# Gating the later loads and interleaving halves of the first V sums with the transposes, in a fused attention and gated-MLP kernel

## The chip, the cores and the metric

One core of a Trainium2 chip runs the whole kernel. The metric is the device time in microseconds of one execution. TensorE (PE in the profile) does matrix products and transposes, VectorE (DVE), ScalarE (ACT) and GpSimd (POOL) do the elementwise work, and SyncE (SP) issues nearly all loads and stores.

## The reference

With x of 2048 tokens by 512 features, all in bfloat16:

```python
xn  = layernorm(x)                                # no scale, no bias, eps 1e-5
q, k, v = split(xn @ wqkv)                        # 32 heads of 16
s   = q @ k.T * 16 ** -0.5, kept where 0 <= i - j < 256
att = softmax(s) @ v @ wo
mlp = ((xn @ w_gate) * (xn @ w_up)) @ w_down      # inner width 1792
out = x + att + mlp
```

## The kernel before

The tokens are worked off in blocks of 128 and in chunks of four blocks. Everything stays on the chip between the loads at the start and the stores of the result. `run` writes the order of all engines out by hand: it calls `setup` and `first_chunk`, then goes through steps of scores (L317), exponentials (L323), masks and values (L370), and between them fills TensorE with projections, gate and up products (L399, L410), down products (L432) and the output product (L438) from a list.

`setup` issues all loads on SyncE's one queue in this order (L74 to L89): x of block 0, of block 1, of blocks 2 and 3; the V, K and Q columns of wqkv (L77, 512 KB each); the first halves of w_gate and w_up; x of blocks 4 to 7; the second halves; w_down; wo; the rest of x. It also calls `keep_busy(40)`, forty products of zeros into a PSUM tile `wps` (L131) that nothing reads, so that TensorE has something to do while the first x lands.

`first_chunk` does chunk 0 by itself. Per block b:

- `norm_stats` (L173, L174) and `norm_scale` (L183, L186) make mean and inverse deviation on VectorE and GpSimd; `norm_apply` (L194) writes the scaled block `xn` on VectorE, one instruction of 512 columns.
- `norm_transpose` (L213) transposes the four 128x128 parts of `xn` on TensorE into a PSUM tile `xTp`, and ScalarE copies them to `xnT` (L214). For block 0 the parts go two by two into two tiles with a copy each; for the others four into one tile with one copy.
- `proj_v` (L243) sums the four products of `xnT` with the V columns of wqkv into a PSUM tile `vp`, and VectorE or ScalarE copies it out to V (L236, L234).

Between the transposes of block 0 and those of block 1 stands `keep_busy(8)`. Then, for b from 0 to 3, the transposes of block b+1 are issued before the V sum of block b:

```python
for b in range(4):
    if b < 3:
        self.norm_transpose(b + 1, False)
    self.proj_v(b, engine="act" if b == 2 else "dve")
    if b == 0:
        self.norm_apply(3)
```

After V come the key and query sums (`proj_qk`, L255), the copy of V with its halves swapped (`swap_halves`, L153) and the list. PSUM tiles of `ps_m` (tag M, four buffers, `wps` among them) are taken in turn; the scores' tile S has four banks of its own.

Of the kernel before, what the change touches and what calls it, by code (L numbers as in the profile page):

```python
# [8 lines left out]
F32 = mybir.dt.float32  # L9
I32 = mybir.dt.int32  # L10
ACT = mybir.ActivationFunctionType
ALU = mybir.AluOpType
# [22 lines left out]
class Kernel:  # L35
# [26 lines left out]
    def setup(self):  # L62
        nc, const, NT, NF = self.nc, self.const, self.NT, self.NF
        self.x = const.tile([128, NT, 512], BF16, name="x")
        self.Wqkv = const.tile([128, 4, 1536], BF16, name="Wqkv")
        self.Wo = const.tile([128, 4, 512], BF16, name="Wo")
        self.Wg = const.tile([128, 4, self.F], BF16, name="Wg")
        self.Wu = const.tile([128, 4, self.F], BF16, name="Wu")
        self.Wd = const.tile([128, NF, 512], BF16, name="Wd")
        xv = self.x_d.rearrange("(t p) d -> p t d", p=128)  # L70
        wq = self.w_d["qkv"].rearrange("(k p) n -> p k n", p=128)
        wg = self.w_d["g"].rearrange("(k p) n -> p k n", p=128)
        wu = self.w_d["u"].rearrange("(k p) n -> p k n", p=128)
        for lo, hi in ((0, 1), (1, 2), (2, 4)):  # L74
            nc.sync.dma_start(out=self.x[:, lo:hi, :], in_=xv[:, lo:hi, :])
        for lo in (1024, 512, 0):
            nc.sync.dma_start(out=self.Wqkv[:, :, lo:lo + 512], in_=wq[:, :, lo:lo + 512])  # L77
        h = self.F // 2
        for lo in (0, h):
            nc.sync.dma_start(out=self.Wg[:, :, lo:lo + h], in_=wg[:, :, lo:lo + h])  # L80
            nc.sync.dma_start(out=self.Wu[:, :, lo:lo + h], in_=wu[:, :, lo:lo + h])
            if lo == 0:
                nc.sync.dma_start(out=self.x[:, 4:8, :], in_=xv[:, 4:8, :])
        nc.sync.dma_start(out=self.Wd[:], in_=self.w_d["d"].rearrange("(f p) n -> p f n", p=128))
        wo = self.w_d["o"].rearrange("(c p) n -> p c n", p=128)
        for c in range(4):
            nc.sync.dma_start(out=self.Wo[:, c, :], in_=wo[:, c, :])
        for lo, hi in ((8, 10), (10, 12), (12, NT)):
            nc.sync.dma_start(out=self.x[:, lo:hi, :], in_=xv[:, lo:hi, :])  # L89

        self.idle = const.tile([128, 128], BF16, name="idle")
        nc.vector.memset(self.idle[:], 0.0)  # L92
        self.keep_busy(40)
        warm = const.tile([128, 1], F32, name="warm")
        nc.vector.memset(warm[:], 0.0)
        nc.scalar.activation(out=warm[:], in_=warm[:], func=ACT.Exp)
        ident = const.tile([128, 128], BF16, name="ident")
        nc.gpsimd.memset(ident[:], 0.0)
        nc.gpsimd.affine_select(out=ident[:], in_=ident[:], compare_op=ALU.not_equal, fill=1.0,
                                base=0, pattern=[[-1, 128]], channel_multiplier=1)  # L100
        self.ident = ident
        pi = const.tile([128, 1], I32, name="pi")
        nc.gpsimd.iota(pi[:], pattern=[[0, 1]], base=0, channel_multiplier=1)
        podd = const.tile([128, 1], I32, name="podd")
        nc.vector.tensor_scalar(out=podd[:], in0=pi[:], scalar1=4, scalar2=1,
                                op0=ALU.arith_shift_right, op1=ALU.bitwise_and)
        self.odd = const.tile([128, 1], F32, name="odd")
        nc.vector.tensor_copy(out=self.odd[:], in_=podd[:])
        self.even = const.tile([128, 1], F32, name="even")
        nc.vector.tensor_scalar(out=self.even[:], in0=self.odd[:], scalar1=-1.0, scalar2=1.0,  # L110
                                op0=ALU.mult, op1=ALU.add)
        self.mhalf = const.tile([128, 4], F32, name="mhalf")
        nc.gpsimd.memset(self.mhalf[:], -0.5)
        self.diag = const.tile([128, 64], BF16, name="diag")
        self.far = const.tile([128, 64], BF16, name="far")
        nc.gpsimd.memset(self.diag[:], BIG)
        nc.gpsimd.memset(self.far[:], BIG)
        for half in (slice(0, 64), slice(64, 128)):
            self.triangle(self.diag[half], True)
            self.triangle(self.far[half], False)  # L120
        self.xnT, self.Q, self.hT, self.OT = {}, {}, {}, {}
        self.K, self.V, self.VS = {}, {}, {}
        self.strips, self.parts, self.at = {}, {}, {}
        self.stock = []
        self.new_values()

    def keep_busy(self, n):

        ps = self.ps_m.tile([128, 128], F32, tag="M", name="wps")
        for _ in range(n):  # L130
            self.nc.tensor.matmul(ps[:], lhsT=self.idle[:], rhs=self.idle[:], start=True, stop=True)  # L131

    def new_chunk(self, T):

# [55 lines left out]
    def norm_apply(self, t):  # L190
        nc = self.nc
        mv, j, rs = self.stats.pop(t)
        xn = self.work.tile([128, 512], BF16, tag="xn", name="xn")
        nc.vector.tensor_scalar(out=xn[:], in0=self.x[:, t, :], scalar1=mv[:, j, 0:1],  # L194
                                scalar2=rs[:, j:j + 1], op0=ALU.subtract, op1=ALU.mult)
        self.book("dve", MASK)
        self.xns[t] = xn

    def norm_transpose(self, t, by_dma):

        nc = self.nc
        xn = self.xns.pop(t)
        T, b = divmod(t, 4)
        if b == 0:
            self.xnT[T] = self.chunk2.tile([128, 4, 4, 128], BF16, tag="xnT", name=f"xnT{T}")
        if by_dma:
            nc.sync.dma_start_transpose(out=self.xnT[T][:, b, :, :], in_=xn[:])
            return
        n = 2 if b == 0 else 4
        for lo in range(0, 4, n):  # L210
            ps = self.ps_m.tile([128, n, 128], BF16, tag="M", name="xTp")
            for k in range(n):
                nc.tensor.transpose(ps[:, k, :], xn[:, 128 * (lo + k):128 * (lo + k) + 128], self.ident[:])  # L213
            nc.scalar.activation(out=self.xnT[T][:, b, lo:lo + n, :], in_=ps[:], func=ACT.Copy)  # L214

    def bank(self, ks, name):

# [54 lines left out]
    def first_chunk(self):  # L272

        self.new_chunk(0)
        for b in range(2):
            self.norm_stats(b, 1)
            self.norm_scale(b, 1)
        for b in (0, 1, 2):
            self.norm_apply(b)
            if b < 2:  # L280
                self.norm_stats(b + 2, 1)
                self.norm_scale(b + 2, 1)
        self.norm_transpose(0, False)
        self.keep_busy(8)
        for b in range(4):
            if b < 3:
                self.norm_transpose(b + 1, False)
            self.proj_v(b, engine="act" if b == 2 else "dve")
            if b == 0:
                self.norm_apply(3)  # L290
        self.proj_qk(0, 0, 1, engine="dve")
        self.proj_qk(0, 0, 0, engine="act")
        self.swap_halves(0, self.nc.scalar)
        self.proj_qk(0, 1, 1, engine="dve")
# [234 lines left out]

    def run(self):  # L530
        self.xns, self.stats, self.sums = {}, {}, {}
        self.pads = 0
        self.now, self.free = 0, dict(act=0, dve=0)
        self.setup()
        NCH = self.NCH
# [17 lines left out]
        spent, n = 0, 0  # L553
# [62 lines left out]
        T = NCH - 1  # L616
# [58 lines left out]
```

The softmax here doesn't subtract the row's maximum and nothing guards it: scores larger than these inputs give would overflow.

## Time and profile before

| | |
|---|---|
| median of 4 runs | 263.44 us (263.27 to 264.25) |
| profiled execution | 263.52 us |
| its span, first to last instruction | 261.5 us |
| TensorE busy | 257.8 us (99%) |
| VectorE, ScalarE, GpSimd busy | 179.5, 176.4, 115.7 us |
| bytes read from HBM | 9.70 MB |
| first V sum, first key sum on TensorE | 6.96, 11.05 us |

Times inside an execution count from its first instruction. A line of the timeline gives start, duration, engine, source line, operation, tile written and tile read, shapes, how many were merged, and in brackets the idle time before and what ended it. "L213" is line 213 of the listing. PE durations include a modelled end, so the distance of two starts, not the duration, is what a product costs in a dense row.

### The profile page before, as it was taken

How to read it: one execution, taken by the hardware profiler on the slowest of the kernel's cores; microseconds unless marked ns; L12 is line 12 of the kernel's file. 1: busy time of each engine (PE TensorE's matmuls, PEld its weight loads, DVE VectorE, ACT ScalarE, POOL GpSimd, SP SyncE). 2: the span in 40 equal slices, each digit the busy share in tenths (PEclk: the TensorE clock that was granted, in tenths of full speed). 3: DMA queues.
4: the chain of work that ended last, by engine and by line, in shares of the span. 5: the costliest groups of instructions: out<-in, count | busy, mean ns of one | idle time of the engine just before them, and what ended most of it. 6: DMA issues, size and time to landing. Idle time of an engine off the chain costs nothing.

```text
span 261.5 us, 7740 instructions
## 1 busy us (share of the span) xinstructions
PE 257.8 (99%) x3170; PEld 118.5 (45%) x3170; DVE 179.5 (69%) x357; ACT 176.4 (67%) x143; POOL 115.7 (44%) x278
## 2 busy tenths in 40 slices
PE   8999999999999999999999999999999999999995
PEld 8444444444444544444544454444544445444453
DVE  6687888879845597557973769767795235977344
ACT  3377788888756866678775567767787546787600
POOL 6215342425457645334456644544443451464600
PEclk9999999999999999999999999999999999999999
DMA  6999920120002300002001310001100100000002
GB/s 194 377 354 338 278 36 20 24 48 1 3 28 34 103 3 1 3 0 48 3 3 40 84 43 3 0 1 25 27 3 0 43 24 20 5 0 3 1 3 83
DMA packets 19427, 15.05 MB, mean 58 GB/s; under 512 B 7360, under 2 KB 19392, under 8 KB 19392
## 3 DMA queue, kind: packets, MB, share of 16 engines
q1 hardware_dynamic: 18848, 14.26, 18.4%
q8 instruction: 26, 0.43, 0.7%
q10 hardware_dynamic: 544, 0.30, 0.4%
q14 instruction: 9, 0.07, 0.1%
HBM read 9.70 MB, written 2.10 MB: 45 GB/s over the span
## 4 chain that ended last, share of the span: by engine, by line
PE 99%; DVE 0%; issue 0%
PE gp L399 19%; PE up L410 19%; PE psd L432 17%; PE qkp L255 11%; PE S L317 9%; PE acc L370 7%; PE vp L243 5%; PE psd L438 5%; PE L L432 2%; PE wps L131 2%; PE L L438 1%; PE xTp L213 1%; PE L L370 0%; DVE x L448 0%; DVE idle L92 0%
## 5 line engine op out<-in xcount | busy, mean ns | idle before, releaser
L323 ACT ACTIVATE P<-S 128x2048 bf16<-128x2048 f32 x75 | 140.7, 1876 | 49.6 <-PE S L317 41.0
L162 POOL TENSOR_SCALAR_AFFINE_SELECT P<-P 64x256 bf16<-64x256 bf16 x224 | 99.4, 444 | 124.4 <-ACT P L323 107.9
L399 PE MATMUL gp<-xnT,Wg 128*128 128x512 bf16 x224 | 60.1, 380 | 0.0
L410 PE MATMUL up<-xnT,Wu 128*128 128x512 bf16 x224 | 59.1, 380 | 0.0
L415 DVE TENSOR_TENSOR hT<-up,gsb 128x512 bf16<-128x512 f32 x56 | 38.3, 685 | 18.3 <-PE up L410 13.1
L432 PE MATMUL psd<-Wd,hT 128*128 128x512 bf16 (+1 forms) x210 | 48.0, 369 | 0.0
L347 DVE TENSOR_TENSOR P<-P,diag 128x512 bf16<-128x512 bf16 (+1 forms) x75 | 29.6, 395 | 5.9 <-ACT P L323 5.9
L432 PEld LDWEIGHTS <-hT 128*128 128x128 bf16 x238 | 21.3, 98 | 25.3 <-issue 3.5
L410 PEld LDWEIGHTS <-Wu 128*128 128x128 bf16 x224 | 20.4, 98 | 25.6 <-issue 3.3
L399 PEld LDWEIGHTS <-Wg 128*128 128x128 bf16 x224 | 20.3, 98 | 25.3 <-issue 3.3
L255 PE MATMUL qkp<-xnT,Wqkv 128*128 128x512 bf16 x128 | 29.9, 380 | 0.0
L317 PE MATMUL S<-Q,K 32*128 32x320 bf16 (+4 forms) x720 | 29.9, 254 | 0.0
L234 ACT ACTIVATE gsb<-gp 128x512 bf16<-128x512 f32 x38 | 22.3, 596 | 7.7 <-PE gp L399 6.9
L317 PEld LDWEIGHTS <-K 32*128 32x128 bf16 x720 | 10.2, 92 | 30.7 <-issue 30.3
L376 DVE STREAM_TRANSPOSE at<-acc 128x512 f32<-128x512 f32 x30 | 19.1, 688 | 6.5 <-PE acc L370 6.4
L448 DVE TENSOR_TENSOR x<-psd,x 128x512 bf16<-128x512 f32 (+1 forms) x15 | 9.7, 655 | 15.7 <-PE psd L438 15.7
L255 PEld LDWEIGHTS <-Wqkv 128*128 128x128 bf16 x128 | 11.7, 98 | 14.6 <-issue 1.8
L370 PE MATMUL acc<-P,VS 64*32 64x320 bf16 (+4 forms) x672 | 17.7, 253 | 0.0
L370 PE MATMUL acc<-P,V 64*32 64x320 bf16 (+4 forms) x672 | 17.5, 253 | 0.0
L370 PEld LDWEIGHTS <-V 64*32 64x32 bf16 x720 | 15.1, 91 | 2.3 <-issue 1.7
L243 PE MATMUL vp<-Wqkv,xnT 128*128 128x512 bf16 x64 | 15.3, 380 | 0.0
L370 PEld LDWEIGHTS <-VS 64*32 64x32 bf16 x720 | 14.7, 91 | 0.6 <-issue 0.2
(54 smaller groups left out, 182.1 us busy)
## 6 DMA issues: line engine op xcount, KB each, us to landing
out_dram<-x SPq DMA_DIRECT2D x15, 128.0 KB, 1.9
Wg<-in_B_w_gate_dram SPq DMA_DIRECT2D x2, 896.0 KB, 11.2
Wu<-in_B_w_up_dram SPq DMA_DIRECT2D x2, 896.0 KB, 12.6
Wd<-in_B_w_down_dram SPq DMA_DIRECT2D x1, 1792.0 KB, 17.9
Wqkv<-in_A_wqkv_dram SPq DMA_DIRECT2D x3, 512.0 KB, 5.7
x<-in_A_x_dram SPq DMA_DIRECT2D x2, 512.0 KB, 8.4
VS<-V SPq DMA_DIRECT2D x6, 144.0 KB, 2.6
x<-in_A_x_dram SPq DMA_DIRECT2D x3, 256.0 KB, 6.6
```

Source lines behind the costliest of these rows:

```text
L162: nc.gpsimd.affine_select(out=v, in_=v, pattern=pattern + [[1 if diag else -1, 64]], compare_op=ALU.is_ge if diag else ALU.is_gt, fill=0.0 ...
L234: nc.scalar.activation(out=out, in_=in_, func=ACT.Copy)
L243: nc.tensor.matmul(ps[:], lhsT=self.xnT[T][:, b, k, :], rhs=self.Wqkv[:, k, 1024:1536], start=(k == 0), stop=(k == 3))
L255: nc.tensor.matmul(ps[:], lhsT=self.Wqkv[:, k, lo:lo + 128], rhs=self.xnT[T][:, :, k, :], start=(k == 0), stop=(k == 3))
L317: nc.tensor.matmul(S[:, e, col:col + n], lhsT=self.K[U, c][rows, keys], rhs=self.Q[T, c][rows, q:q + n], start=True, stop=True, tile_posit ...
L323: nc.scalar.activation(out=P[:, :, 0:col], in_=S[:, :, 0:col], func=ACT.Exp, scale=0.25)
L347: self.nc.vector.tensor_tensor(out=v, in0=v, op=ALU.min, in1=self.diag.unsqueeze(1).unsqueeze(1).to_broadcast([128, 4, n, 64]))
L370: nc.tensor.matmul(accs[par][32 * e:32 * e + 32, q:q + n], lhsT=v, rhs=P[rows, e, col:col + n], start=(i == 0), stop=(i == len(todo) - 1), ...
L399: nc.tensor.matmul(ps[:], lhsT=self.Wg[:, k, 128 * f:128 * f + 128], rhs=self.xnT[T][:, :, k, :], start=(k == 0), stop=(k == 3))
L410: nc.tensor.matmul(ps[:], lhsT=self.Wu[:, k, 128 * f:128 * f + 128], rhs=self.xnT[T][:, :, k, :], start=(k == 0), stop=(k == 3))
L415: nc.vector.tensor_tensor(out=self.hT[T, f][:], in0=ps[:], in1=self.gsb[:], op=ALU.mult)
L432: nc.tensor.matmul(ps, lhsT=self.hT[T, f][:, 128 * b:128 * b + 128], rhs=self.Wd[:, f, c0:c1], start=(f == 0), stop=False)
```

## The change

Three things change in the first chunk; the rest of the program is the same.

- Of the loads, only x of blocks 0 to 3 and the V columns are issued in `setup`. All others move, in the same order, to `later_loads`, called after the statistics of block 0. It first has ScalarE copy one element of block 0's mean into the first K column of `Wqkv`; the K load overwrites that column, so it waits for the copy, and on SyncE's queue all later loads stand behind it.
- `norm_apply(0)` is two instructions of 256 columns. Every transposed block is copied to `xnT` in two instructions of two parts; those of blocks 1 to 3 read one PSUM tile.
- The V sum of block b is split: its first two products, then the transposes of block b+1, then the last two. `keep_busy(8)` becomes `keep_busy(6)`, and `keep_busy(2)` is put behind V sum 0. The fillers write one tile of the scores' pool in place of tiles of `ps_m`.

```diff
 (setup)
         for lo, hi in ((0, 1), (1, 2), (2, 4)):
             nc.sync.dma_start(out=self.x[:, lo:hi, :], in_=xv[:, lo:hi, :])
-        for lo in (1024, 512, 0):
-            nc.sync.dma_start(out=self.Wqkv[:, :, lo:lo + 512], in_=wq[:, :, lo:lo + 512])
...
+        nc.sync.dma_start(out=self.Wqkv[:, :, 1024:1536], in_=wq[:, :, 1024:1536])
         self.idle = const.tile([128, 128], BF16, name="idle")
         nc.vector.memset(self.idle[:], 0.0)
         self.keep_busy(40)
+    def later_loads(self, go):
...
+        nc.scalar.activation(out=self.Wqkv[:, 0, 512:513], in_=go, func=ACT.Copy)
+        for lo in (512, 0):
+            nc.sync.dma_start(out=self.Wqkv[:, :, lo:lo + 512], in_=wq[:, :, lo:lo + 512])
+        h = self.F // 2
+        for lo in (0, h):
+            nc.sync.dma_start(out=self.Wg[:, :, lo:lo + h], in_=wg[:, :, lo:lo + h])
+            nc.sync.dma_start(out=self.Wu[:, :, lo:lo + h], in_=wu[:, :, lo:lo + h])
+            if lo == 0:
+                nc.sync.dma_start(out=self.x[:, 4:8, :], in_=xv[:, 4:8, :])
...
     def keep_busy(self, n):
-        ps = self.ps_m.tile([128, 128], F32, tag="M", name="wps")
+        if self.spare is None:
+            self.spare = self.s_tiles.tile([128, 4, 512], F32, tag="S", name="wps")
         for _ in range(n):
-            self.nc.tensor.matmul(ps[:], lhsT=self.idle[:], rhs=self.idle[:], start=True, stop=True)
+            self.nc.tensor.matmul(self.spare[:, 0, 0:128], lhsT=self.idle[:], rhs=self.idle[:], start=True, stop=True)
 (norm_apply)
-        nc.vector.tensor_scalar(out=xn[:], in0=self.x[:, t, :], scalar1=mv[:, j, 0:1],
-                                scalar2=rs[:, j:j + 1], op0=ALU.subtract, op1=ALU.mult)
+        n = 256 if t == 0 else 512
+        for lo in range(0, 512, n):
+            nc.vector.tensor_scalar(out=xn[:, lo:lo + n], in0=self.x[:, t, lo:lo + n], scalar1=mv[:, j, 0:1],
+                                    scalar2=rs[:, j:j + 1], op0=ALU.subtract, op1=ALU.mult)
 (norm_transpose)
-            nc.scalar.activation(out=self.xnT[T][:, b, lo:lo + n, :], in_=ps[:], func=ACT.Copy)
+            for k in range(0, n, 2):
+                nc.scalar.activation(out=self.xnT[T][:, b, lo + k:lo + k + 2, :], in_=ps[:, k:k + 2, :], func=ACT.Copy)
 (first_chunk)
             self.norm_stats(b, 1)
+            if b == 0:
+                self.later_loads(self.mv[:, 0, 0:1])
             self.norm_scale(b, 1)
...
         self.norm_transpose(0, False)
-        self.keep_busy(8)
-        for b in range(4):
-            if b < 3:
-                self.norm_transpose(b + 1, False)
-            self.proj_v(b, engine="act" if b == 2 else "dve")
-            if b == 0:
-                self.norm_apply(3)
+        self.keep_busy(6)
+        self.proj_v(0, (0, 1))
+        self.norm_transpose(1, False)
+        self.proj_v(0, (2, 3), engine="dve")
+        self.keep_busy(2)
+        self.norm_apply(3)
+        self.proj_v(1, (0, 1))
+        self.norm_transpose(2, False)
+        self.proj_v(1, (2, 3), engine="dve")
+        self.proj_v(2, (0, 1))
+        self.norm_transpose(3, False)
+        self.proj_v(2, (2, 3), engine="act")
+        self.proj_v(3, engine="dve")
```

More of the change, by code (lines that the diff above doesn't have):

```diff
@@ L71, in setup @@
         wq = self.w_d["qkv"].rearrange("(k p) n -> p k n", p=128)
-        wg = self.w_d["g"].rearrange("(k p) n -> p k n", p=128)
-        wu = self.w_d["u"].rearrange("(k p) n -> p k n", p=128)
         for lo, hi in ((0, 1), (1, 2), (2, 4)):
             nc.sync.dma_start(out=self.x[:, lo:hi, :], in_=xv[:, lo:hi, :])
-        for lo in (1024, 512, 0):
[L77 to L89, printed above, removed]
+        nc.sync.dma_start(out=self.Wqkv[:, :, 1024:1536], in_=wq[:, :, 1024:1536])
         self.idle = const.tile([128, 128], BF16, name="idle")
@@ L125, in setup @@
         self.new_values()
+    def later_loads(self, go):
+        nc, NT = self.nc, self.NT
+        xv = self.x_d.rearrange("(t p) d -> p t d", p=128)
+        wq, wg, wu = (self.w_d[k].rearrange("(k p) n -> p k n", p=128) for k in ("qkv", "g", "u"))
+        nc.scalar.activation(out=self.Wqkv[:, 0, 512:513], in_=go, func=ACT.Copy)
[7 more added lines that the diff above has]
+                nc.sync.dma_start(out=self.x[:, 4:8, :], in_=xv[:, 4:8, :])
+        nc.sync.dma_start(out=self.Wd[:], in_=self.w_d["d"].rearrange("(f p) n -> p f n", p=128))
+        wo = self.w_d["o"].rearrange("(c p) n -> p c n", p=128)
+        for c in range(4):
+            nc.sync.dma_start(out=self.Wo[:, c, :], in_=wo[:, c, :])
+        for lo, hi in ((8, 10), (10, 12), (12, NT)):
+            nc.sync.dma_start(out=self.x[:, lo:hi, :], in_=xv[:, lo:hi, :])
     def keep_busy(self, n):
-        ps = self.ps_m.tile([128, 128], F32, tag="M", name="wps")
+        if self.spare is None:
+            self.spare = self.s_tiles.tile([128, 4, 512], F32, tag="S", name="wps")
         for _ in range(n):
-            self.nc.tensor.matmul(ps[:], lhsT=self.idle[:], rhs=self.idle[:], start=True, stop=True)
+            self.nc.tensor.matmul(self.spare[:, 0, 0:128], lhsT=self.idle[:], rhs=self.idle[:], start=True, stop=True)
     def new_chunk(self, T):
@@ L531, in run @@
         self.xns, self.stats, self.sums = {}, {}, {}
-        self.pads = 0
+        self.pads, self.spare = 0, None
         self.now, self.free = 0, dict(act=0, dve=0)
```

## The prediction

> **What bounds the kernel now.** I read the page first, then the chain of waits, then the timeline of the first 26 us, then the answers for the tiles Wqkv, Wg and xnT, then busy time by stretch. From the page:
>
> ```profile
> PE 257.8 (99%) x3170; PEld 118.5 (45%) x3170; DVE 179.5 (69%) x357; ACT 176.4 (67%) x143; POOL 115.7 (44%) x278
> PEclk9999999999999999999999999999999999999999
> PE 99%; DVE 0%; issue 0%
> ```
>
> TensorE is busy from end to end and the chain that ended last runs on it alone. So the time is "when the first V sum starts" plus "the work behind it". Busy by stretch says the second term has no holes:
>
> ```profile
> 11.05:30.00 18.95, 18.95 (x163) 7.90 (x169) 15.25 (x30) 12.40 (x12) 5.95 (x18) 1.00 1.06 344
> 30.00:60.00 30.00, 30.00 (x412) 13.26 (x388) 24.74 (x50) 25.55 (x24) 11.40 (x26) 1.00 0.21 48
> ```
>
> From 11.05 us, the start of the first key sum (L255), TensorE has 18.95 busy in 18.95 and 30.00 in 30.00. The change touches only what lies before 11.05, so all it can win or lose is the shift of that point, unless a late load makes a new hole. The prologue, from the timeline:
>
> ```profile
> 1.04 4.45 PE L131 MATMUL wps<-idle 128*128 128x128 bf16 x40 [1.04 <-DVE warm L95]
> 4.77 0.38 DVE L194 TENSOR_SCALAR xn<-x,mv,rs 128x512 bf16<-128x512 bf16 x1
> 5.28 0.63 PE L213 MATMUL xTp<-ident,xn 128*128 128x128 bf16 x4
> 5.71 1.06 PE L131 MATMUL wps<-idle 128*128 128x128 bf16 x8
> 5.73 0.66 ACT L214 ACTIVATE xnT<-xTp 128x256 bf16<-128x256 bf16 x2 [3.45 <-PE xTp L213]
> 6.56 0.56 PE L213 MATMUL xTp<-ident,xn 128*128 128x128 bf16 x4
> 6.96 1.03 PE L243 MATMUL vp<-Wqkv,xnT 128*128 128x512 bf16 x4
> 7.82 0.39 PE L213 MATMUL xTp<-ident,xn 128*128 128x128 bf16 x4
> 8.24 0.60 ACT L214 ACTIVATE xnT<-xTp 128x512 bf16<-128x512 bf16 x1 [0.49 <-PE xTp L213]
> 8.63 0.41 DVE L194 TENSOR_SCALAR xn<-x,mv,rs 128x512 bf16<-128x512 bf16 x1
> 9.09 0.23 PEld L213 LDWEIGHTS <-xn 128*128 128x128 bf16 x4 [0.51 <-DVE xn L194]
> 11.05 2.75 PE L255 MATMUL qkp<-xnT,Wqkv 128*128 128x512 bf16 x12
> ```
>
> Useful sums begin at 6.96; everything TensorE did before is filler (wps) or transposes. Between 6.96 and 11.05 lie 16 V sums, the transposes of blocks 2 and 3, and one hole: V sum 1 gives out at 8.91, and the transposes of block 3 wait until 9.09 for its scaled block (0.18). Though the clock row says full speed throughout, the steps do not. Starts of the four transposes of block 0 are (0.63 - 0.31) / 3 = 0.107 apart, those of block 2 (0.39 - 0.22) / 3 = 0.056: before about 6.8 every TensorE step takes twice as long. A V sum steps by (1.03 - 0.38) / 3 = 0.216 at the fast rate, so 0.43 at the slow one. The V weights:
>
> ```profile
> L77 SPq DMA_DIRECT2D Wqkv<-in_A_wqkv_dram x3: 470/508/513, 2.2 to 3.2; - x3
> DMA to landing us min/median/max: 4.2/5.7/6.6
> ```
>
> Issued at 2.17, 2.68 and 3.23, the V, K and Q columns land at 6.36, 8.35 and 9.84. V's landing is 0.6 before its first use, but that use moves forward.
>
> **The change, part by part.** The profiled execution took 263.52 (span 261.5, 2.0 outside), 0.08 above the median 263.44. I work out when the first key sum starts, against 11.05.
>
> *Gate.* The statistics of block 0 are ready at 3.85 (L174, 3.66 + 0.18). ScalarE idles from 2.28 to 5.73, so the one-element copy runs at once; the nearest row is L96's 128x1 ACTIVATE, 0.20. The K load is issued near 4.15 instead of 2.68. Queued behind it on SP are Q, Wg, Wu, x, Wd, Wo and the rest, each up to 1.5 later. Who waits: K at about 11 (8.35 + 1.5 = 9.85 at worst), Q at 11.9 (11.3 at worst), the first Wg half at 18.8 (12.2 + 1.5), the first Wu half at 19.7 (14.7 + 1.5), x blocks 4 to 7 at 23.5 (17.5 + 1.5). The second Wg half is not read before 30 and lands at 20.8. All are covered, the tightest, Q, by 0.6, and that bound assumes the whole 1.5 reaches the landing; while V is still landing until about 6 the engines have work, so I expect near 0.5. Price: nothing. Gain: V alone in the queue. The x blocks 2 and 3 land at 4.6; the 512 KB of V at 350 GB/s (the rate of the stretches around 7 to 9) are 1.5 more, with receipt hardly before 5.7. So V lands between 5.7 and 6.36; I take 6.1, since packets of a queue mostly go in order and K's stood behind V's already.
>
> The Trainium skill (DMA: Bandwidth & Descriptors, Rules for kernel authors) advises the reverse of a gate: issue a load early and wait late. By that rule the issue shift of 1.5 would be a loss; the landings with 1.5 added, above, make it none.
>
> *Block 0 scaled in halves.* Two DVE instructions for one of 0.38. Bounds for the pair: 0.38 to twice 0.38; nearest is ScalarE's split, two halves in 0.66 where a whole takes 0.60, so I take +0.06. The first half is ready near 5.0, but the 40 fillers hold TensorE until 5.28, where the whole block was ready already (5.15). Gain nothing; cost 0.06 on DVE, hidden: block 1's scaled tile is needed at about 7.0 and is there at 6.4.
>
> *Six fillers for eight, then the first half of V sum 0 ahead of block 1's transposes.* Fillers end at 5.71 + 6 x 0.107 = 6.35. The first copied half is there at about 6.12, the weights at 6.1 plus some 0.2 for wait and weight load. So V sum 0 starts at 6.35 instead of 6.96. One step is at the slow rate (0.43), one fast (0.22): 7.00. Transposes of block 1 (4 x 0.056): 7.22. Second half of V sum 0: 7.65. Two fillers: 7.76.
>
> *Copies in halves.* Half a V block (0.43) is all that now lies between the end of a block's transposes and its own first sums, where a whole (0.86) lay. From the first of four transposes: two transposes end after 0.056 + 0.22, ScalarE starts 0.04 later, the half takes 0.38, the weight load 0.06: 0.75. Covered: 0.22 + 0.43 = 0.65, and 0.76 for block 1 with the two fillers. So 0.10 is lost at block 2 and 0.10 at block 3, none at block 1. The second half of the copy is 0.28 behind the first (6.01 against 5.73), under the 0.43 of the sums before it.
>
> *Sum.* V 1 first half 7.76 to 8.19, transposes 2 to 8.42, V 1 second half to 8.85, wait 0.10, V 2 first half to 9.38, transposes 3 to 9.60 (V 0's eviction 7.85 to 8.54, scaled block 3 at about 8.9: the 0.18 hole is gone), V 2 second half to 10.03, wait 0.10, V 3 to 10.99. Against 11.05 that is -0.06. In terms: start -0.61, hole -0.18, block 1's transposes now behind the start +0.22, slow step +0.21, fillers +0.11, copy waits +0.20; total -0.05. ScalarE's three extra copies and the filler's move to the S banks lie on no path.
>
> The unknowns: weights at 6.36 start V sum 0 at 6.54, +0.1; weights at 5.7 gain nothing while the six slow fillers run until 6.35. If the fast rate comes earlier, at 6.1 say, the same count with fast steps from there ends at 10.74 for the kernel before and 10.66 for the changed one; at 5.3, at 10.7 and 10.4. So the shift is -0.4 to +0.1, and I take -0.15, nearer the computed row than the end: 263.44 - 0.15 = 263.3. Own range 263.0 to 263.6.
>
> The Trainium skill (TensorE: Matmul & The Clock Gate, What's actually happening) says the gate counts activity in a free-running window of about 3.4 us, so the switch need not fall at 6.8 in each run; one profile can't show that. As an estimate from that page, with fillers from 1.04 on, the switch could fall from 4.45 to 7.9, and the last would turn the shift into about +0.1.
>
> **Rivals.**
> *The gate's full worth.* V lands by 5.7 and the fast rate comes by 5.3. Then the limit is the scaled blocks: block 1's at 6.4 lets its transposes end at 6.68, and the order above ends at 10.4, or 10.25 without the copy waits: -0.65 to -0.8, 262.6 to 262.8. For it: 0.6 of filler before V's landing. Against: the slow steps until 6.8.
> *ScalarE's copy becomes the bound (slower).* Place: between each block's transposes and its first sums. If the halves are waited for as a whole (all four transposes first, then both copies), 0.75 becomes 0.75 + 0.11 + 0.28 = 1.14 against 0.65 to 0.76 covered: 0.38 + 0.49 + 0.49 = 1.36 instead of 0.20, so +1.1, 264.5. It decides from 0.65 after the first transpose on. Against: block 0's two copies start 0.28 apart already and its V sum waited for neither.
> *A gated load is late.* Q past 11.9 stops TensorE at 1:1; landing 1.5 later still leaves 0.6, so the delay must exceed 2.1, and 2.9 gives +0.8, 264.2. No row speaks for so much.
> *The gate does nothing*: V at 6.36, about 263.5, within the first case.
>
> **How the numbers follow.** 0.3% is 0.8 us, about what a measurement of this kernel can tell from no change. First case 0.54, all within. Full worth 0.30: its price ends at that bound, and block 1's scaled block, on which it hangs, may come 0.1 earlier or later, so I put 0.18 past the bound and 0.12 within. Copy bound 0.11, late load 0.05, all slower. Faster 0.18, same 0.66, slower 0.16. The range leaves out the copy case and the last tenth of full worth: 262.5 to 264.2.
>
> **What would show it.** Right: first V sum at 6.3 to 6.4, V weights at about 6.1, K's issue at 4.1 to 4.2, no wait of block 3's transposes for xn, two waits near 0.1 on ScalarE's copies, first key sum near 11.0, the rest full. Wrong: key sums before 10.4 (the gate or the rate does more), waits of 0.4 on xnT (copies), or a TensorE wait on a load after 11.

## The result and the profile after

The changed kernel takes 263.76 us (median of 41 runs, 263.53 to 264.47), the kernel before 263.35 (64 runs, 263.12 to 265.18): a ratio of 1.0014, interval 1.0009 to 1.0019. That is 0.4 us slower. The size is within the 0.8 us that the forecast called no change, but 263.76 lies above its range of 263.0 to 263.6: the sign is the other one, and the interval excludes none. The profiled execution took 263.67, its span is 261.6.

From the page, the two rows that answer to those of before (busy time of each engine, and the engines of the chain that ended last):

```profile
PE 257.5 (98%) x3170; PEld 117.8 (45%) x3170; DVE 179.7 (69%) x358; ACT 176.7 (68%) x147; POOL 115.5 (44%) x278
PE 98%; ACT 0%; DVE 0%; issue 0%
```

TensorE still carries everything, now with holes of its own: 98% instead of 99%, and ScalarE has come into the chain. Busy by stretch (stretch, its length, then each engine's busy time) shows that they are not behind the prologue:

```profile
11.05:30.00 18.95, 18.95 (x156) 7.81 (x161) 15.16 (x30) 12.31 (x11) 5.95 (x18) 1.00 1.08 351
30.00:60.00 30.00, 30.00 (x409) 13.27 (x394) 24.76 (x50) 25.55 (x24) 11.28 (x26) 1.00 0.24 48
```

So no gated load came late. The prologue, from the timeline:

```profile
4.12 0.92 SPq L118 DMA_DIRECT2D Wqkv<-in_A_wqkv_dram  x2
4.78 0.57 DVE L202 TENSOR_SCALAR xn<-x,mv,rs 128x256 bf16<-128x256 bf16 x2
5.28 0.47 PE L221 MATMUL xTp<-ident,xn 128*128 128x128 bf16 x4
5.58 0.50 PE L137 MATMUL wps<-idle 128*128 128x128 bf16 x6
6.37 0.59 PE L252 MATMUL vp<-Wqkv,xnT 128*128 128x512 bf16 x2 [0.29 <-ACT xnT L223]
6.80 0.39 PE L221 MATMUL xTp<-ident,xn 128*128 128x128 bf16 x4
7.23 0.66 ACT L223 ACTIVATE xnT<-xTp 128x256 bf16<-128x256 bf16 x2 [0.90 <-PE xTp L221]
7.46 0.27 PE L137 MATMUL wps<-idle 128*128 128x128 bf16 x2
7.66 0.61 PE L252 MATMUL vp<-Wqkv,xnT 128*128 128x512 bf16 x2
8.11 0.39 PE L221 MATMUL xTp<-ident,xn 128*128 128x128 bf16 x4
8.33 1.24 PE L252 MATMUL vp<-Wqkv,xnT 128*128 128x512 bf16 x4
8.53 0.66 ACT L223 ACTIVATE xnT<-xTp 128x256 bf16<-128x256 bf16 x2 [0.65 <-PE xTp L221]
9.63 1.68 PE L252 MATMUL vp<-Wqkv,xnT 128*128 128x512 bf16 x6
11.14 2.75 PE L264 MATMUL qkp<-xnT,Wqkv 128*128 128x512 bf16 x12
```

Three things are to be seen. The first V sum starts at 6.37, 0.59 earlier than before, and still TensorE stood idle ahead of it: the fillers are through at 5.58 + 6 x 0.056 = 5.92. The 0.29 idle is put down to ScalarE, but its first half copy had ended at 6.06; what came in last are the V columns, issued at 2.17. The view of the tile Wqkv gives the time from issue to landing of its three loads, and the shortest, V's, is 4.2:

```profile
DMA to landing us min/median/max: 4.2/4.6/5.6
```

Unrounded it is 4.16, a landing at 6.33, against 6.36 before. Second, the copies of block 1 start at 7.23, when all four transposes are through (6.80 + 0.39 = 7.19), not after two; those of block 2 do the same (8.11 + 0.39 = 8.50, start at 8.53). Third, the V sums have holes: four products in a dense row take 3 x 0.216 + 0.38 = 1.03, and the row at 8.33 takes 1.24; six take 1.46, and the row at 9.63 takes 1.68. With the 0.09 between the fillers' end (7.57) and 7.66 that makes waits of 0.09, 0.21 and 0.22, all on the half copy. The first key sum starts at 11.14, 0.09 after that of the kernel before.

That start is the whole time: profiled time less start of the first key sum is 252.47 before, 252.53 after, and 252.47 to 252.70 in nine of the ten experiments below (252.95 in e5_banks_nofill, whose profiled execution is one of the two slowest of its eleven: TensorE's last product ends there at 258.75, against 258.94 in the changed kernel, and what follows it takes 0.4 longer). Whatever a version does is read at this one place.

### The profile page after: what moved, and what is told of

Its sections match the earlier page's. It is cut to its first block, busy times and chain, and to the rows that moved or that the text cites. A ratio compares the mean times of both kernels' runs of the same rounds, so it can differ in the third digit from the quotient of the medians.

```text
span 261.6 us, 7744 instructions
## 1 busy us (share of the span) xinstructions
PE 257.5 (98%) x3170; PEld 117.8 (45%) x3170; DVE 179.7 (69%) x358; ACT 176.7 (68%) x147; POOL 115.5 (44%) x278
## 4 chain that ended last, share of the span: by engine, by line
PE 98%; ACT 0%; DVE 0%; issue 0%
PE gp L416 19%; PE up L427 19%; PE psd L449 17%; PE qkp L264 11%; PE S L334 9%; PE acc L387 7%; PE vp L252 6%; PE psd L455 5%; PE L L449 2%; PE wps L137 2%; PE L L455 1%; PE L L387 0%; PE xTp L221 0%; ACT xnT L223 0%; DVE x L465 0%
## 5 line engine op out<-in xcount | busy, mean ns | idle before, releaser
L252 PE MATMUL vp<-Wqkv,xnT 128*128 128x512 bf16 x64 | 16.0, 380 | 0.4 <-ACT xnT L223 0.3
## 6 DMA issues: line engine op xcount, KB each, us to landing
Wg<-in_B_w_gate_dram SPq DMA_DIRECT2D x2, 896.0 KB, 10.4
```

The costliest lines, as they stand in the source:

```text
L252: nc.tensor.matmul(ps[:], lhsT=self.xnT[T][:, b, k, :], rhs=self.Wqkv[:, k, 1024:1536], start=(k == 0), stop=(k == 3))
```

## Experiments

Theory A: the interleaved order costs more than it saves, because half a V sum does not cover transposes and copy of the next block, and the earlier start is stopped by the landing of the V columns. Theory B: the gate or the halved instructions cost the time. The runs of the kernel before that stand beside them have medians of 263.36 (e1 to e4), 263.42 (e5 to e8) and 263.30 (e9 and e10). Line numbers differ from version to version; operations and tiles do not.

**The order undone (e1_order).**

```diff
-        (six fillers, V sums split around the next transposes)
+        self.keep_busy(8)
+        for b in range(4):
+            if b < 3:
+                self.norm_transpose(b + 1, False)
+            self.proj_v(b, engine="act" if b == 2 else "dve")
...
```

> The changed kernel with the order of before put back: eight fillers, then the transposes of block b+1 ahead of the whole V sum of block b; gate, halved scaling and halved copies stay. Theory A (the interleaving costs more than it saves, because half a V sum does not cover the transposes and copies of the next block): the three waits of 0.10, 0.21 and 0.21 us on ScalarE's copies go, the first V sum goes back behind block 1's transposes, and the time is within 0.15 us of the kernel before, about 263.4. Theory B (the gate or the halved instructions cost the time): it stays near 263.8.

Measured 263.42, ratio 0.9999 (0.9990 to 1.0008): back to before, with the gate and all halved instructions still in. From its timeline:

```profile
1.04 3.77 PE L137 MATMUL wps<-idle 128*128 128x128 bf16 x40 [1.04 <-DVE warm L79]
6.51 0.40 PE L221 MATMUL xTp<-ident,xn 128*128 128x128 bf16 x4 [0.39 <-DVE xn L202]
6.74 1.03 PE L252 MATMUL vp<-Wqkv,xnT 128*128 128x512 bf16 x3
9.11 1.89 PE L252 MATMUL vp<-Wqkv,xnT 128*128 128x512 bf16 x8
10.84 1.24 PE L264 MATMUL qkp<-xnT,Wqkv 128*128 128x512 bf16 x5
```

Two dense V sums take 7 x 0.216 + 0.38 = 1.89: no hole in the last eight. This is also the fair row to hold the change against, since TensorE has its fast rate before the first V sum here as in the changed kernel's profile. The starts of its 128-column steps go from 0.107 to 0.056 apart at about 3.9 here (the forty fillers take 3.77 in place of 4.45), at 5.4 in the changed kernel and at 6.9 in the kernel before. From first V sum to first key sum it has 10.84 - 6.74 = 4.10: 16 x 0.216 = 3.46 of sums, 8 x 0.056 = 0.45 of transposes, 0.19 of waits for scaled blocks. The changed kernel has 4.77: 3.46, then 0.67 for twelve transposes, 0.11 of fillers and 0.53 of waits. It starts 0.37 sooner, pays 0.22 + 0.11 + 0.34 for it, and ends 0.30 later.

**The gate alone, and the change without it (e4_gate, e3_nogate).**

```diff
 (e4_gate: the kernel before)
-        (all loads in setup)
+            self.norm_stats(b, 1)
+            if b == 0:
+                self.later_loads(self.mv[:, 0, 0:1])
```

> The kernel before with the gate alone. Theory A: no change from before, 263.35 within 0.1 us. Theory B (the gate costs): about 263.75. If an earlier landing of the V columns were worth something by itself: below 263.2.

Measured 263.31, ratio 0.9997 (0.9988 to 1.0005): in the order of before the gate shows neither a gain nor a cost.

```diff
 (e3_nogate: the changed kernel)
-        nc.scalar.activation(out=self.Wqkv[:, 0, 512:513], in_=go, func=ACT.Copy)
-            if b == 0:
-                self.later_loads(self.mv[:, 0, 0:1])
+        self.later_loads(None)                       # in setup
```

> The changed kernel without the gate: all loads are issued at the start as before, no one-element copy. Theory A: the V columns land within 0.05 us of 6.33 either way, so the first V sum starts at the same time and the time stays within 0.1 us of 263.75. Theory B (the gate costs): back to about 263.4. If the gate helps after all: V lands later than 6.4 and the time goes up by as much.

Measured 264.06 (seven runs), ratio 1.0026 (1.0015 to 1.0036): slower still, against both theories as I had put them, and as the third case had it. Its timeline has

```profile
6.73 0.40 PE L252 MATMUL vp<-Wqkv,xnT 128*128 128x512 bf16 x1 [0.17 <-DMA Wqkv<-in_A_wqkv_dram]
11.52 0.59 PE L264 MATMUL qkp<-xnT,Wqkv 128*128 128x512 bf16 x2
```

and V landed at 6.68, not 6.36. In the changed order V sum 0 stands right behind that landing, and 0.35 later there is the later key sum (11.52 against 11.14, 0.03 of it from the slow rate's last step). So the gate does not cost the changed order its time, and seems to save it some 0.3; e10_banks_nogate below comes back to that.

**Another tile and bank for the second pair of transposes (e2_banks, e5_banks_nofill).** ScalarE's first copy waited for transposes it does not read. Here the second pair goes to another PSUM tile: `spare`, one tile of four banks, of which block b uses bank b.

```diff
+        for lo in (0, 2):
+            if b and lo:
+                ps = self.spare[:, b, 0:256].rearrange("p (k n) -> p k n", k=2)
+            else:
+                ps = self.ps_m.tile([128, 2, 128], BF16, tag="M", name="xTp")
+            for k in range(2):
...
+            nc.scalar.activation(out=self.xnT[T][:, b, lo:lo + 2, :], in_=ps[:, 0:2, :], func=ACT.Copy)
```

> The changed kernel with the second pair of each later block's transposes in a PSUM bank of its own (one of the four scores banks; the late fillers become transposes of the zeros into the first of these), so that the first half copy shares no bank with a transpose still to come. Theory A: the copy starts 0.11 us after two transposes instead of after four, the waits of 0.10, 0.21 and 0.21 become about 0, 0.10 and 0.10, and the time falls by 0.3 to about 263.45. If the copies wait for the whole block for another reason, or the waits are not on the path: no change, 263.75.

Measured 263.76, ratio 1.0015 (1.0007 to 1.0024): no gain, though the waits at blocks 2 and 3 fell as expected. What took it back is in my edit:

```profile
7.41 0.38 ACT L228 ACTIVATE xnT<-xTs 128x256 bf16<-128x256 bf16 x1
7.84 0.27 PE L141 MATMUL xTs<-ident,idle 128*128 128x128 bf16 x2 [0.20 <-ACT xnT L228]
8.61 1.13 PE L257 MATMUL vp<-Wqkv,xnT 128*128 128x512 bf16 x4
```

The third row is 0.10 over dense, where it was 0.21. But the two fillers behind V sum 0 write the tile that ScalarE was copying, and stood until 7.84, when that copy (7.41 + 0.38 = 7.79) was through. They write bank 0 of the tile and the copy reads its bank 1, so here the program waits for a whole tile, across banks. The next version drops the fillers.

```diff
-        self.keep_busy(2)
```

> The changed kernel with the second pair of each later block's transposes in a bank of its own, as in e2_banks, but without the two fillers behind V sum 0, which in e2_banks waited 0.37 us for ScalarE's copy of the tile they share. Theory A (the wait between a block's transposes and its copy is what the interleaving costs): waits of about 0.10 at each of blocks 1 to 3, first key sum near 10.8 instead of 11.15, time 263.35 to 263.45, no slower than before. Rival (the loss lies elsewhere in the interleaving, the two-bank form is of no use): 263.75.

Measured 263.42, ratio 0.9999 (0.9989 to 1.0008): the whole loss is gone, with the interleaved order kept. Its TensorE and ScalarE rows:

```profile
6.96 0.27 PE L227 MATMUL xTp<-ident,xn 128*128 128x128 bf16 x2
7.27 0.38 ACT L228 ACTIVATE xnT<-xTp 128x256 bf16<-128x256 bf16 x1 [1.21 <-PE xTp L227]
7.19 1.13 PE L257 MATMUL vp<-Wqkv,xnT 128*128 128x512 bf16 x4
8.38 1.13 PE L257 MATMUL vp<-Wqkv,xnT 128*128 128x512 bf16 x4
9.57 1.56 PE L257 MATMUL vp<-Wqkv,xnT 128*128 128x512 bf16 x6
```

The copy starts 0.04 after the first pair (7.23), while the second pair, begun at 7.07, is still under way. All three waits are 0.10, which is what the forecast had reckoned for blocks 2 and 3. Two things changed together, though. The fillers alone were not dropped: by the changed kernel's rows their 0.11 would only have been added to block 1's wait of 0.09 (an estimate). And the second pair got another tile as well as another bank, so these runs don't say which of the two frees the copy; the fillers of e2_banks speak for the tile.

**The copies whole again (e6_whole).**

```diff
-            for k in range(0, n, 2):
-                nc.scalar.activation(out=self.xnT[T][:, b, lo + k:lo + k + 2, :], in_=ps[:, k:k + 2, :], func=ACT.Copy)
+            nc.scalar.activation(out=self.xnT[T][:, b, lo:lo + n, :], in_=ps[:], func=ACT.Copy)
```

> The changed kernel with the copies of blocks 1 to 3 whole again (one of 512 columns). Theory A: the first product of blocks 1 to 3 waits for 0.60 in place of 0.38 us of copy, the waits become 0.32, 0.43 and 0.43, and the time rises by 0.65 to about 264.4. If a copy had to be complete before the first product anyway, so that halving brought nothing: no change or a little faster, 263.6 to 263.75.

Measured 264.55 (five runs), ratio 1.0037 (1.0024 to 1.0051). The waits became 0.31 to 0.43, as expected; V landed at 6.58 in this profile, so its first V sum starts 0.25 later besides:

```profile
9.65 0.60 PE L251 MATMUL vp<-Wqkv,xnT 128*128 128x512 bf16 x2 [0.26 <-ACT xnT L222]
11.16 0.82 PE L251 MATMUL vp<-Wqkv,xnT 128*128 128x512 bf16 x3 [0.26 <-ACT xnT L222]
```

So the halves are used one by one, and the change's own halving saves the interleaved order about 0.65 of its waits. What was left of them is what it lost.

**The V columns in two transfers (e7_vsplit), and all remedies together (e8_best).**

```diff
-        nc.sync.dma_start(out=self.Wqkv[:, :, 1024:1536], in_=wq[:, :, 1024:1536])
+        for k in (0, 2):
+            nc.sync.dma_start(out=self.Wqkv[:, k:k + 2, 1024:1536], in_=wq[:, k:k + 2, 1024:1536])
 (e8_best: also the two banks, no late fillers, and in norm_apply)
-        n = 256 if t == 0 else 512
+        n = 512
```

> The changed kernel with the V columns loaded in two transfers of two row groups each, of which the first two V products need the first alone. Theory A (the first V sum stands at the landing of the V columns, 6.33, and 0.04 later): the first half lands near 5.6, V sum 0 starts at 5.9 to 6.0 behind the fillers and the first copy, block 1's transposes start when its scaled block is there, at 6.5 instead of 6.8, and the time falls by 0.25 to about 263.5. If the waits behind it take the gain back, or the half lands no earlier: 263.75.

Measured 263.66, ratio 1.0006 (0.9997 to 1.0014): a gain of 0.1 in the median rather than 0.25, which this run can't tell from none. The first half landed at 6.11 in this profile, not at 5.6; x blocks 2 and 3, ahead of it in the queue, were late too, at 5.35 where e8_best has 4.58.

> The changed kernel with the two banks without late fillers, the V columns in two transfers, and block 0 scaled whole again, so that block 1's scaled block is ready 0.13 us earlier (6.34). Theory A: the three gains add up, first key sum near 10.4, time about 263.0, faster than before by 0.3. If only one of them is on the path at a time: 263.3 to 263.4.

Measured 263.29, ratio 0.9995 (0.9986 to 1.0004): not distinguishable from before, and nearer to what was expected if only one gain at a time is on the path than to 263.0. In the profiled execution, which took 263.11, the half landed at 5.47 and all went as expected:

```profile
5.96 0.60 PE L258 MATMUL vp<-Wqkv,xnT 128*128 128x512 bf16 x2
10.41 1.67 PE L270 MATMUL qkp<-xnT,Wqkv 128*128 128x512 bf16 x7
```

But its eleven runs spread from 262.96 to 263.96. The likely reason, not shown for the unprofiled runs, is the landing, which lay at 6.11 and 5.47 in the two profiles.

**The V columns ahead of x blocks 2 and 3 (e9_vfirst), and e5_banks_nofill without the gate (e10_banks_nogate).**

```diff
 (e9_vfirst: order of the first loads)
-  x 0, x 1, x 2 and 3, first half of V, second half of V
+  x 0, x 1, first half of V, x 2 and 3, second half of V
```

> The kernel of e8_best with the first half of the V columns loaded ahead of x blocks 2 and 3. Theory A (the start of V sum 0 follows the landing of its columns, which varied from 6.33 to 6.69 between profiles of kernels that load them last): the first half lands near 5.0 and never decides any more, x blocks 2 and 3 land near 5.4 and delay block 2's statistics by at most 0.2 us, which is covered; first key sum near 10.4 in every run, time 263.1, faster than before by 0.2 to 0.3. If block 2's later statistics decide: 263.4 or more.

Measured 263.68, ratio 1.0014 (1.0006 to 1.0023): a miss. The half landed at 5.45, no earlier than in e8_best, and x blocks 2 and 3 at 6.16 instead of 4.58. VectorE waits for them in front of block 1's scaling, so block 1 came late:

```profile
6.18 0.69 DVE L184 BATCH_NORM_STATS2 st<-x 128x6 f32<-128x512 bf16 x1 [1.05 <-DMA x<-in_A_x_dram]
7.45 0.28 PE L228 MATMUL xTp<-ident,xn 128*128 128x128 bf16 x2 [0.71 <-DVE xn L207]
```

> The kernel of e5_banks_nofill without the gate: all loads at the start, no one-element copy. If the gate is worth something only where the V sum stands right behind the landing of its columns (as the difference of e3_nogate to the changed kernel suggests): V lands near 6.7 and the time rises by 0.3 to about 263.7. If that difference was chance: 263.4.

Measured 263.76, ratio 1.0015 (1.0006 to 1.0024) against 0.9999 with the gate. V landed at 6.77 and V sum 0 started at 6.82:

```profile
6.82 0.59 PE L257 MATMUL vp<-Wqkv,xnT 128*128 128x512 bf16 x2 [0.71 <-DMA Wqkv<-in_A_wqkv_dram]
```

Both pairs with and without the gate differ by 0.3 us in the median. The intervals of each pair just overlap. The landings of V in one piece (6.33, 6.35, 6.33, 6.49 and 6.58 in gated profiles, 6.36, 6.68 and 6.77 in ungated ones) go the same way, but in two pieces its last one landed at 6.74, 6.13 and 6.83 with the gate (e7 to e9). So I take the gain as likely and not as shown; nor is it shown why V should land later beside the loads behind it.

## Why the prediction was wrong

The frame held: only the start of the first key sum matters, the rest stays dense, no gated load is late. The forecast for that start was 0.15 earlier; it is 0.30 later than with the order undone, and the medians are 0.4 apart. My sum ended at 10.99 and the profile has 11.14: the waits were 0.32 longer than in the sum, and the slow step that it had in V sum 0 (0.21) did not occur.

**The copies in halves: the step that failed.** I reckoned 0.75 from a block's first transpose to its first V product, with the copy starting after two transposes. It starts after four: from 8.11 to the copy's start at 8.53 are 0.42 instead of 0.32, and to the product 0.86. The waits were sized 0, 0.10 and 0.10 and measured 0.09, 0.21 and 0.22; that is 0.32 more than the sum had. With the second pair in another tile and bank they are 0.10 each. My slower rival named the right place and was half right: all four transposes are waited for, but not both copies, so it cost 0.3 more than my sum and not 1.16. I had argued against it from block 0, whose two copies start 0.28 apart; but block 0 has two tiles, and that was the very difference. The Trainium skill (PSUM — Partial Sum Buffer, PSUM bank collisions raise a hardware error) says that two engines must not touch the same 32 partitions of one bank at once, at different addresses either, and that waits are therefore to be set by bank rather than by address. The start after four transposes in one bank (0.42), and after two with a second (0.31), agrees with that rule, which would have pointed to this wait. It isn't shown that the bank is what the program waited for: the fillers of e2_banks waited across banks of one tile.

**The landing of V.** Taken at 6.1 between 5.7, for which I had no row, and 6.36, measured at 6.33, and 6.33 to 6.58 in the other gated profiles that load V in one piece. The upper bound was one reading, of a kernel where nothing hung on it; ungated it reached 6.77. The first V sum did start at 6.37, but by chance: the fillers that I had ending at 6.35 were over at 5.92, and the 0.2 that I had put between landing and first product was 0.04. That is why an earlier fast rate gave the change nothing, where I had it win 0.1 to 0.3. The 10.4 that I gave for a fast rate from 5.3 on did not follow from my own terms: with V at 6.1 and 0.2 behind it, the first V sum starts at 6.3, and the sum ends at 10.7, no better than the kernel before. The gain of 0.3 in that case, and with it most of the lower end of my shift, hung on it.

**The row compared with.** The forecast compared with the profiled execution of before, whose TensorE was slow until 6.9. With an earlier fast rate the old order starts the V sums at 6.74 (e1_order) and 6.82 (e4_gate) rather than 6.96, and the median is 0.17 below that execution. The changed kernel, held by a landing, has no such gain. In the twelve profiles the steps change from 0.107 to 0.056 at times from 3.9 (e1_order) to 6.9. The Trainium skill (TensorE: Matmul & The Clock Gate, What's actually happening) has the switch depend on where in a free-running window the first product falls, and gives ±500 ns for it. That it varies agrees; but the times here are 3 us apart, and 3.9 is earlier than the 4.45 of my estimate from that page. The measurement decides.

**The gate.** "Nothing" was right in the old order (0.9997) and probably wrong in the new, where both kernels without it were about 0.3 slower. The Trainium skill's advice to issue loads early (DMA: Bandwidth & Descriptors, Rules for kernel authors) is not borne out for the loads behind V here: issued 1.4 later they cost nothing.

**What came as forecast.** K is issued at 4.12, block 3's transposes no longer wait for their scaled block, the halved scaling of block 0 is hidden behind the order (though it took 0.57 where I had 0.44, against 0.38 for the whole, and block 1 was ready at 6.47 instead of 6.34), and the transposes and fillers now behind the start cost their 0.22 and 0.11.

Open stay the reason for V's later landing beside other loads, and how much of the runs' spread is landing and how much the fast rate.

## What to carry to other kernels

Splitting a sum around the next block's transposes halves the cover of the copy in between, so reckon the copy's whole path, from the first transpose to the first product, against the half that is left. Here the copy of half a PSUM tile started only when the last of the four writes to that tile was through: if halves are to overlap, give each half a tile of its own, in a bank of its own. And when work is moved up to right behind a load, its start is the landing: take several readings of that landing, not one.

## What the runs showed of the hardware

A 256 KB half of the V columns does not land in a time that its size or place in the queue fixes: 6.11 and 5.47 in two profiles with the same first loads (e7_vsplit, e8_best), and 5.45 when issued 0.47 earlier (e9_vfirst). In the profile with 6.11 the load ahead of it was late as well, 5.35 against 4.58, so the delay is not the V load's alone. In e9_vfirst x blocks 2 and 3, as large, went from 4.58 to 6.16 when issued 0.47 later.

The first product behind a landing starts 0.04 to 0.05 after it: 6.33 and 6.37 in the changed kernel, 6.77 and 6.82 in e10_banks_nogate.
